# Weight gradients of a two-branch attention layer: transposes and gates at other places, two small gradients in one pass

## The chip, the cores and the metric

The kernel runs on one core of one Trainium2 chip. A core has a matrix engine (TensorE, PE in the profile, with its weight loads as PEld), a vector engine (VectorE, DVE), a scalar engine (ScalarE, ACT), a general engine (GpSimd, POOL) and a queue engine (SyncE, SP) that here only issues transfers. GpSimd issues transfers too. The transfers run on 16 DMA engines that all queues share. Each engine works through its own instructions in order; semaphores tie the engines together. The metric is the device time of one execution in microseconds (us).

## The reference

The reference computes a layer and all its gradients. For x (2048 tokens, 576 wide), the output is g * a + (1 - g) * b, where g is a sigmoid gate per token, a is attention with 32 query heads of 18 and one shared key and value head, and b is attention with 32 heads of 128 over 64 segments of 32 tokens, each with 8 memory rows that are handed on from segment to segment:

```
def _fwd_reference(A_x, A_wq, A_wk, A_wv, A_wo, B_x, B_mem0, B_Wq, B_Wk, B_Wv, B_Wo, B_seg_len, gate_w):
    ...
    g = _sigmoid((x * gate_w).sum(-1, keepdims=True))
    a = _A_ref(x, A_wq, A_wk, A_wv, A_wo)
    b = _B_ref(x, B_mem0, B_Wq, B_Wk, B_Wv, B_Wo, B_seg_len)
    return g * a + (1 - g) * b

def reference(A_x, ..., B_x, B_seg_len, grad_out):
    ...
    _out, _vjp = jax.vjp(_f, A_x, A_wq, A_wk, A_wv, A_wo, B_mem0, B_Wq, B_Wk, B_Wv, B_Wo, gate_w)
    return (out, *_vjp(grad_out))
```

The work around the change is the last of it: the gradients of the four large weights of branch b (each 576 x 4096), which are sums over 2048 tokens and 512 memory rows; the output itself with the gradient of the gate; and then the gradients of x and of the small weights of branch a (576 x 576 and 576 x 18).

## The kernel before, in words

The kernel runs in stages, one after the other: preparation, projections, the forward chain over segments woven with the first pass of branch a, the bulk of branch b, the backward chain woven with the second pass of branch a, a closing pass (`b_post`), the weight gradients (`b_dw`), and the final stage (`a_final`). The change lies in the last two. Their order of instructions is written out by hand (`manual_schedule`) in `b_dw`; in `a_final` a planner reorders what doesn't depend on each other.

`b_dw` has 16 sets, k = 0 to 15: four gradients (o, dq, dk, dv) times four pairs of 512 columns. A set's two tiles (w_d, for k = 0 w_a and w_b) have 20 blocks of 128 rows: 16 of tokens and 4 of memory rows. `load(k + 1)` is issued on SyncE at the head of set k; two tile pools alternate, so it waits until set k - 1 has released its tiles. For k < 4 the memory rows come by transposing transfers (`dma_start_transpose`). `groups` yields after every group: for k < 4 eight groups of 40 products of 288 columns, each in two accumulators, for k >= 4 eight groups of 20 products of 512 columns and a ninth in which the last 64 rows of both tiles run side by side (40 products, 64 columns of the array each). The accumulators (w_acc, six buffers) are evicted by VectorE and ScalarE in turn (`evac`), and the results leave by GpSimd's queue.

Between groups stands one step of a generator, `mem_tok`. It is made anew at k = 0, 4 and 8 and brings the memory rows' gradients (dq, dk, dv) into rows by token. Its start issues two loads (z_src, SyncE). Then for each of four blocks there is one step in which VectorE and GpSimd copy a half each (z_v, L612) and the next load but one is issued, and four steps of eight transposes on TensorE (z_pt), evicted to z_tk; the fourth writes the block to memory by GpSimd's queue (L623). So twenty steps, of which sixteen have work for TensorE. What is written for dq is read by `load(4)`.

At each set's end stands `gate(k)` for the token block k: ten products on TensorE (o_T by w_wo), then on VectorE the difference to branch b (o_diff), the output (o_out), the sum for the gate's gradient and its share of dz_all. Its inputs are fetched by `gate_load(k)` at the head of the set, behind `load(k + 1)`: o_b and o_go on GpSimd's queue, and o_T by a transposing transfer on SyncE's queue (L968). Each has one buffer, so the next set's fetch waits until this set's gate has read it. At k = 1 SyncE also fetches hx, the token and memory rows that serve from k = 4 on, ahead of o_T. After k = 15 dz_all is cast (w_dz) and 32 products give the gradient of gate_w (L1536 to L1545), and two large loads for the final stage (`ot`, `da`) are issued.

`a_final` first makes dx for each of 16 token blocks. Then, for each of five blocks of weight rows (four of 128, one of 64), it sums two gradients over 16 token blocks with `row_mm` (512 and 64 columns, accumulator f_big), evicts them and writes them by SyncE's queue (L2184), and a third, small one (f_pk), which the planner puts earlier.

Of the kernel before, what the change touches and what calls it, by code (L numbers as in the profile page):

```python
# [12 lines left out]
BF16 = mybir.dt.bfloat16  # L13
F32 = mybir.dt.float32
U16 = mybir.dt.uint16
U32 = mybir.dt.uint32
P = 128

D = 576
# [27 lines left out]
class Kern:  # L47
# [1381 lines left out]
    def b_dw(self, sp, A, wB, wH, ht, psum):  # L1429
        nc = self.nc  # L1430
        NTT = self.NTT
# [3 lines left out]
        def load(k):  # L1435
            which, jp = WS[k // 4], k % 4
            ts = []
            if k == 0:
                tiles = [[pA.tile([P, 4, 512], BF16, name=f"w_{w}{j}", bufs=1) for j in range(n // 4)] for w in "ba"][::-1]
            else:  # L1440
                tiles, full[k] = [], []
                for _ in range(2):
                    t = (wB if k % 2 else pA).tile([P, n, 512], BF16, name="w_d", bufs=2)
                    full[k].append(t)
                    tiles.append([t[:, j:j + 4, :] for j in range(0, n, 4)])
            for jc in (2 * jp, 2 * jp + 1):
                cs = slice(jc * 512, (jc + 1) * 512)
                t = tiles.pop(0)
                src = self.xtok[which][0:self.T, cs].rearrange("(n p) d -> p n d", p=P)
                if k == 0:  # L1450
                    for j in range(NTT // 4):
                        nc.sync.dma_start(t[j][:], src[:, 4 * j:4 * j + 4, :])
                else:
                    nc.sync.dma_start(full[k][jc % 2][:, 0:NTT, :], src)
                ts.append((t, cs))
                if k < 4:
                    for mt in range(self.NM // P):
                        nc.sync.dma_start_transpose(
                            t[NTT // 4][:, mt, :].rearrange("p (h e) -> p h e", e=E),
                            self.oh_dram[mt][:, 4 * jc:4 * jc + 4, :].rearrange("e h t -> e (h t)"))  # L1460
                else:
                    nc.sync.dma_start(t[NTT // 4][:, :, :], self.mtok[which][:, cs].rearrange("(n p) d -> p n d", p=P))
            return ts
# [40 lines left out]
        with self.tc.manual_schedule():  # L1504
            self.load_h(None, self.dm_dram, wH, ht)
            full = {}
            hold = ExitStack()
            pA = A("wA0", hold)
            nxt = load(0)
            wo = sp.tile([P, NKT, D], BF16, name="w_wo", bufs=1)  # L1510
            nc.vector.memset(wo[64:128, 4, :], 0.0)
            nc.gpsimd.dma_start(wo[:, 0:4, :], self.A_wo[0:512, :].rearrange("(k p) d -> p k d", p=P))
            nc.gpsimd.dma_start(wo[0:64, 4, :], self.A_wo[512:D, :])
            mem = None
            for k in range(16):
                ts = nxt
                if k % 4 == 0 and k < 12:
                    mem = self.mem_tok(k // 4, sp, psum, 2)
                    next(mem)
                if k == 1:  # L1520
                    hold.close()
                    pA = A("wA")
                if k < 15:
                    nxt = load(k + 1)
                if k == 1:
                    hx = self.load_h(self.A_x, self.mem_dram, sp)
                gl = self.gate_load(k, sp)
                if k == 15:
                    self.final_load(pA, wH)
                for _ in groups(k, ts, ht):  # L1530
                    next(mem, None)
                self.gate(k, gl, wo, sp, psum)
                if k == 3:
                    ht = hx
            dz16 = sp.tile([P, NTT], BF16, name="w_dz", bufs=1)
            nc.vector.tensor_copy(dz16[:], self.dz_all[:])  # L1536
            pg = [psum.tile([P, 512], F32, name="w_acc", bufs=6) for _ in range(2)]
            for tt in range(NTT):
                for hf in range(2):
                    self.mm(pg[hf][0:1, 0:288], lhsT=dz16[:, tt:tt + 1], rhs=ht[:, tt, 288 * hf:288 * hf + 288],  # L1540
                            start=(tt == 0), stop=(tt == NTT - 1))
            dg16 = sp.tile([P, 2, 288], BF16, name="w_dg", bufs=1)
            for hf in range(2):
                nc.vector.tensor_copy(dg16[0:1, hf, :], pg[hf][0:1, 0:288])
            nc.sync.dma_start(self.outs[11][None, :], dg16[0:1].rearrange("p a b -> p (a b)"))  # L1545
            self.ftok["x"] = ht
            self.final_tok(wB, ("ot", "da"))
# [590 lines left out]
    def a_final(self, sp, psum):  # L2138
        nc = self.nc
        T, NTT = self.T, self.NTT  # L2140
        gwb, wq, wkv, dkv = self.fin
        tok = self.ftok
        wqT = sp.tile([P, NKT, D], BF16, name="f_wqT", bufs=1)
        wkvT = sp.tile([P, D], BF16, name="f_wkvT", bufs=1)
        for kd in range(NKT):
            drows = KT_ROWS[kd]
            ptr = psum.tile([P, 640], BF16, name="f_wtr", bufs=1)
            for kt in range(NKT):
                rows = KT_ROWS[kt]
                self.tr(ptr[0:drows, kt * P:kt * P + rows], wq[0:rows, kt, kd * P:kd * P + drows], rows)  # L2150
            self.evac(wqT[0:drows, kd, :], ptr[0:drows, 0:D])
        ptr = psum.tile([P, 640], BF16, name="f_wtr", bufs=1)
        for kt in range(NKT):
            rows = KT_ROWS[kt]
            self.tr(ptr[:, kt * P:kt * P + rows], wkv[0:rows, kt, :], rows)
        self.evac(wkvT[:, :], ptr[:, 0:D])
        dkt = sp.tile([P, NTT, 36], BF16, name="f_dkt", bufs=1)
        for t4 in range(NTT // 4):
            pk = psum.tile([P, 4, 36], F32, name="f_pk", bufs=1)
            for j in range(4):  # L2160
                tt = t4 * 4 + j
                self.mm(pk[:, j, :], lhsT=dkv[:, tt * P:(tt + 1) * P], rhs=self.selkv[:, :])
            self.evac(dkt[:, t4 * 4:t4 * 4 + 4, :], pk[:])
        for tt in range(NTT):
            trows = slice(tt * P, (tt + 1) * P)
            dqT = self.tok_T(tok["dq"][:, tt, :], sp, psum, "f")
            pdx = psum.tile([P, 640], F32, name="f_big", bufs=2)
            self.row_mm(pdx, [(dqT[0:KT_ROWS[kt], kt, :], wqT[0:KT_ROWS[kt], kt, :]) for kt in range(NKT)]
                        + [(dkv[:, trows], wkvT[:, :])])
            dx32 = sp.tile([P, D], F32, name="f_dx32", bufs=2)  # L2170
            nc.vector.scalar_tensor_tensor(out=dx32[:, :], in0=gwb[:, :], scalar=self.dz_all[:, tt:tt + 1],
                                           in1=pdx[:, 0:D], op0=ALU.mult, op1=ALU.add)
            dx16 = sp.tile([P, D], BF16, name="f_dx16", bufs=2)
            nc.gpsimd.tensor_tensor(out=dx16[:, :], in0=dx32[:, :], in1=tok["dxb"][:, tt, :], op=ALU.add)
            (nc.sync if tt % 2 == 0 else nc.gpsimd).dma_start(self.outs[1][trows, :], dx16[:, :])
        for kt in range(NKT):
            drows = KT_ROWS[kt]
            cs = slice(kt * P, kt * P + drows)
            for (l, r, o) in (("x", "dq", 2), ("ot", "da", 5)):
                pw = psum.tile([P, 640], F32, name="f_big", bufs=2)  # L2180
                self.row_mm(pw[0:drows], [(tok[l][:, tt, cs], tok[r][:, tt, :]) for tt in range(NTT)])
                o16 = sp.tile([P, D], BF16, name="f_o16", bufs=2)
                self.evac(o16[0:drows, :], pw[0:drows, 0:D])
                nc.sync.dma_start(self.outs[o][cs, :], o16[0:drows, :])  # L2184
            pk = psum.tile([P, 4, 36], F32, name="f_pk", bufs=1)
            for tt in range(NTT):
                self.mm(pk[0:drows, 0, :], lhsT=tok["x"][:, tt, cs], rhs=dkt[:, tt, :], start=(tt == 0),
                        stop=(tt == NTT - 1))
            k16 = sp.tile([P, 36], BF16, name="f_k16", bufs=2)
            self.evac(k16[0:drows, :], pk[0:drows, 0, :])  # L2190
            nc.gpsimd.dma_start(self.outs[3][cs, :], k16[0:drows, 0:DA])
            nc.gpsimd.dma_start(self.outs[4][cs, :], k16[0:drows, DA:36])
# [159 lines left out]
```

## Time and profile before

| | us |
|---|---|
| median of three runs | 5294.08 |
| lowest and highest | 5291.89, 5295.3 |
| the profiled execution | 5284.42 |
| its span in the profile | 5282.7 |

| engine | busy us (share of the span) |
|---|---|
| PE | 4991.7 (94%) |
| DVE | 3589.8 (68%) |
| ACT | 3293.3 (62%) |
| POOL | 2553.9 (48%) |

The page shows one profiled execution. Times in its rows count from the start of the span. In a row of the timeline the first number is the start, the second the time until the last of the merged instructions ended, then follow engine, line, operation, the tile written and those read, sizes, count, and in brackets the engine's idle time before it with what ended it. Rows with SPq are SyncE issuing transfers; their time holds what the issue itself waited for, not the transfer. Matmuls overlap, so a group's time is best read from start to start. The stage `b_dw` begins at 4495.93 us in these rows, and `a_final` at 5187.23.

### The profile page before, as it was taken

The page shows a single profiled execution, that of the slowest core. Times are in us where ns is not written, and L with a number is a line of the kernel's source. Part 1 is how long each engine was busy: PE and PEld are TensorE (multiplying, and loading weights), DVE is VectorE, ACT ScalarE, POOL GpSimd, SP SyncE. Part 2 cuts the span into 40 slices and gives each one's busy share as a digit, 9 for nine tenths or more (in the row PEclk, how much of TensorE's full clock was granted, in tenths as well). Part 3 has the DMA queues.
Part 4 walks back from the last instruction along what each step waited for, and adds up shares of the span by engine and source line. Part 5 has one row for each costly group of instructions (what it writes and reads, how often), then busy time and mean ns, then how long its engine had stood idle before and what let it go on. Part 6 is the DMA issues. An engine that isn't in the chain of part 4 may idle for free.

```text
span 5282.7 us, 213348 instructions
## 1 busy us (share of the span) xinstructions
PE 4991.7 (94%) x90766; PEld 2902.2 (55%) x90945; DVE 3589.8 (68%) x7122; ACT 3293.3 (62%) x4757; POOL 2553.9 (48%) x4852
## 2 busy tenths in 40 slices
PE   7999999999999998999889999999999999999998
PEld 4335555555555555777645555555554467764444
DVE  5338888888888887777678888888888831111112
ACT  4228888888888885666668888888877732111100
POOL 3005555555555555767646666666654421222223
PEclk9999999999999999999999999999999999999999
DMA  7755666655665446888866989989877678966663
GB/s 227 241 193 134 145 143 140 146 139 139 146 141 128 121 105 193 254 245 250 264 171 179 201 195 198 198 202 198 201 163 148 139 178 221 275 221 213 195 184 102
DMA packets 1120042, 961.15 MB, mean 182 GB/s; under 512 B 689966, under 2 KB 948023, under 8 KB 1109486
## 3 DMA queue, kind: packets, MB, share of 16 engines
q1 hardware_dynamic: 1020398, 709.26, 54.6%
q0 software_dynamic: 98544, 238.08, 15.0%
q8 instruction: 712, 11.67, 1.0%
q14 instruction: 244, 2.00, 0.1%
q10 hardware_dynamic: 144, 0.15, 0.0%
HBM read 521.16 MB, written 357.96 MB: 166 GB/s over the span
## 4 chain that ended last, share of the span: by engine, by line
PE 69%; ACT 9%; issue 8%; DVE 5%; DMA 4%; POOL 4%; SPq 1%; POOLq 0%; ACTq 0%; DVEq 0%
PE w_acc L82 12%; PE r_pj L82 7%; PE b_S L82 6%; PE a_S L82 6%; PE a_acc L82 5%; ACT b_E L2052 5%; PE c_pj L82 5%; PE b_acc L82 5%; PE r_x L82 5%; PE p_pb L82 4%; PE c_x L82 4%; ACT a_E L1879 3%; PE x_tr L87 2%; PE f_big L82 1%; PE x_po L82 1%
## 5 line engine op out<-in xcount | busy, mean ns | idle before, releaser
L2075 DVE TENSOR_TENSOR b_dS<-b_dP,b_E 128x512 bf16<-128x512 f32 x2048 | 1315.1, 684 | 220.5 <-issue 88.9
L1912 DVE TENSOR_TENSOR a_W<-a_dP,a_E 128x512 bf16<-128x512 f32 x2048 | 1313.9, 684 | 204.6 <-issue 76.2
L2052 ACT ACTIVATE b_E<-b_S 128x1024 bf16<-128x1024 f32 x1024 | 1047.8, 1023 | 286.5 <-PE b_dP L82 200.4
L1879 ACT ACTIVATE a_E<-a_S 128x1024 bf16<-128x1024 f32 x1024 | 1049.0, 1024 | 237.2 <-PE a_dP L82 193.3
L82 PEld LDWEIGHTS <-b_QS 32*128 32x128 bf16 (+1 forms) x8192 | 271.4, 92 | 522.1 <-issue 466.3
L82 PE MATMUL r_pj<-WT,r_dT 128*32 128x288 bf16 x12288 | 495.6, 286 | 3.9 <-issue 3.9
L82 PE MATMUL b_S<-b_KV,b_QS 32*128 32x512 bf16 x2048 | 404.6, 382 | 94.3 <-ACT b_E L2052 60.9
L82 PE MATMUL w_acc<-w_d,w_h 128*128 128x512 bf16 (+1 forms) x2352 | 470.9, 379 | 2.5
L82 PE MATMUL a_S<-a_QD,l_KV 32*128 32x512 bf16 x2048 | 399.3, 381 | 41.6 <-ACT a_E L1879 19.8
L82 PE MATMUL b_acc<-b_dS,b_QS 128*32 128x512 bf16 x2048 | 423.5, 392 | 0.1
L82 PE MATMUL a_acc<-a_E,l_VK 128*32 128x256 bf16 x8192 | 412.3, 278 | 5.0
L82 PE MATMUL b_acc<-b_E,b_QS 128*32 128x512 bf16 x2048 | 405.9, 393 | 0.0
L82 PE MATMUL b_dP<-b_KV,b_QS 32*128 32x512 bf16 x2048 | 402.1, 387 | 0.0
L82 PE MATMUL a_dP<-a_QD,l_KV 32*128 32x512 bf16 x2048 | 398.4, 385 | 0.2 <-DVE a_W L1912 0.2
L82 PEld LDWEIGHTS <-r_dT 128*32 128x32 bf16 x12288 | 336.4, 97 | 93.3 <-issue 6.6
L82 PEld LDWEIGHTS <-w_h 128*128 128x128 bf16 (+1 forms) x2688 | 229.9, 100 | 258.5 <-issue 6.8
L82 PEld LDWEIGHTS <-l_KV 32*128 32x128 bf16 x4096 | 149.9, 91 | 287.0 <-issue 263.5
L82 PE MATMUL a_acc<-a_W,l_WK 128*32 128x256 bf16 x4096 | 291.5, 273 | 0.4 <-DVE a_W L1912 0.3
L79 ACT CAST w_o<-w_acc 128x512 bf16<-128x512 f32 x54 | 31.6, 585 | 384.7 <-PE w_acc L82 371.7
L82 PEld LDWEIGHTS <-l_VK 128*32 128x32 bf16 x8192 | 129.0, 94 | 237.1 <-issue 233.3
L77 DVE CAST w_o<-w_acc 128x512 bf16<-128x512 f32 x54 | 37.3, 692 | 325.2 <-PE w_acc L82 276.6
L1100 POOL TENSOR_TENSOR r_kb<-r_ks,bmask 128x512 bf16<-128x512 bf16 x176 | 188.7, 1072 | 103.7 <-DMA r_ks<-dsx_dram 39.2
(488 smaller groups left out, 10527.9 us busy)
## 6 DMA issues: line engine op xcount, KB each, us to landing
b_QS<-qs_dram SPq DMA_DIRECT2D x256, 256.0 KB
dOx_dram<-p_tok SPq DMA_DIRECT2D x16, 1024.0 KB
c_vx<-vx_dram SPq DMA_DIRECT2D x64, 256.0 KB
krow_dram<-c_k POOLq DMA_DIRECT2D x64, 256.0 KB
qrow_dram<-c_q POOLq DMA_DIRECT2D x64, 256.0 KB
vrow_dram<-c_v POOLq DMA_DIRECT2D x64, 256.0 KB
x_q<-qx_dram SPq DMA_DIRECT2D x32, 512.0 KB
x_k<-kx_dram SPq DMA_DIRECT2D x32, 512.0 KB
```

The source lines that it names most:

```text
L77: nc.vector.tensor_copy(out, in_)
L79: nc.scalar.copy(out, in_)
L82: return self.nc.tensor.matmul(out, lhsT, rhs, start=start, stop=stop, tile_position=tp, skip_group_check=True)
L87: return self.nc.tensor.transpose(out, in_, self.identB[b:b + nrows, b:b + nrows], tile_position=tp)
L1100: nc.gpsimd.tensor_tensor(out=B[:], in0=a[:].unsqueeze(2).to_broadcast([P, 4, 4, SEG]), in1=self.bmask[:, :, 0].unsqueeze(1).unsqueeze(3). ...
L1879: nc.scalar.activation(E_[n][:], S.pop(n)[:], ACT.Exp, scale=SCALEA)
L1912: nc.vector.tensor_tensor(out=W_[n][:, i, :], in0=dP[i][:], in1=E_[n][:, i, :], op=ALU.mult)
L2052: nc.scalar.activation(E_[n][:], S.pop(n)[:], ACT.Exp, scale=SCALEA)
L2075: nc.vector.tensor_tensor(out=D_[n][:, i, :], in0=dP[i][:], in1=E_[n][:, i, :], op=ALU.mult)
```

## The change

Three edits. In set 0 the first three groups are no longer followed by a step of `mem_tok`, so all its twenty steps for dq come three groups later (five in set 0, eight in set 1, seven in set 2, where there were eight, eight and four). For k = 1 to 15 `gate(k)` stands behind the seventh group's step instead of at the end: one group earlier for k < 4, two groups earlier for k >= 4; for k = 0 it stays behind the eighth. In the final stage the 64-row block's two gradients are computed into the two halves of one accumulator, by products that alternate between the two column halves of the array, with one eviction and one output each on SyncE's and on GpSimd's queue.

```
-                for _ in groups(k, ts, ht):
-                    next(mem, None)
-                self.gate(k, gl, wo, sp, psum)
+                for i, _ in enumerate(groups(k, ts, ht)):
+                    if k or i > 2:
+                        next(mem, None)
+                    if i == 7 - (k > 0):
+                        self.gate(k, gl, wo, sp, psum)
                 if k == 3:
                     ht = hx
...
+        pairs = (("x", "dq", 2), ("ot", "da", 5))
         for kt in range(NKT):
             drows = KT_ROWS[kt]
             cs = slice(kt * P, kt * P + drows)
-            for (l, r, o) in (("x", "dq", 2), ("ot", "da", 5)):
+            if drows == 64:
+                pw = psum.tile([P, 640], F32, name="f_big", bufs=2)
+                for c in (slice(0, 512), slice(512, D)):
+                    for tt in range(NTT):
+                        for i, (l, r, o) in enumerate(pairs):
+                            self.mm(pw[64 * i:64 * i + 64, c], lhsT=tok[l][:, tt, cs], rhs=tok[r][:, tt, c],
+                                    start=(tt == 0), stop=(tt == NTT - 1), tp=(0, 64 * i))
+                o16 = sp.tile([P, D], BF16, name="f_o16", bufs=2)
+                self.evac(o16[:], pw[:, 0:D])
+                for i, (l, r, o) in enumerate(pairs):
+                    (nc.sync, nc.gpsimd)[i].dma_start(self.outs[o][cs, :], o16[64 * i:64 * i + 64, :])
+            for (l, r, o) in pairs if drows == P else ():
                 pw = psum.tile([P, 640], F32, name="f_big", bufs=2)
```

With the change, SyncE's queue differs in one place: the load of the dq generator's fourth block stands behind k = 1's o_T instead of behind k = 0's.

## Prediction

> **What bounds the kernel now.** I read the page first, then the chain that ended last, then, stage by stage, TensorE's and SyncE's rows in order of time in the last 800 us, where all edits lie.
>
> ```profile
> PE 4991.7 (94%) x90766; PEld 2902.2 (55%) x90945; DVE 3589.8 (68%) x7122; ACT 3293.3 (62%) x4757; POOL 2553.9 (48%) x4852
> PE w_acc L82 12%; PE r_pj L82 7%; PE b_S L82 6%; PE a_S L82 6%; PE a_acc L82 5%; ACT b_E L2052 5%; PE c_pj L82 5%; PE b_acc L82 5%; PE r_x L82 5%; PE p_pb L82 4%; PE c_x L82 4%; ACT a_E L1879 3%; PE x_tr L87 2%; PE f_big L82 1%; PE x_po L82 1%
> ```
>
> TensorE is busy 94% of the span, and the weight gradients' products (w_acc) are the largest part of the chain. So an edit in that stage is worth what it takes from or adds to TensorE's idle time, its clock, or its number of passes. Its rows at the start of the stage:
>
> ```profile
> 4495.93 9.96 PE L82 MATMUL w_acc<-w_h,w_a 128*128 128x288 bf16 x80
> 4514.80 0.61 PE L87 MATMUL z_pt<-identB,z_v 128*128 128x128 bf16 x4 [8.91 <-DVE z_v L612]
> 4516.55 0.61 PE L87 MATMUL z_pt<-identB,z_v 128*128 128x128 bf16 x4 [1.14 <-POOL z_v L612]
> 4516.95 6.67 PE L82 MATMUL w_acc<-w_h,w_a 128*128 128x288 bf16 x40
> 4523.45 0.61 PE L87 MATMUL z_pt<-identB,z_v 128*128 128x128 bf16 x8
> 4523.90 5.06 PE L82 MATMUL w_acc<-w_h,w_a 128*128 128x288 bf16 x40
> 4528.80 0.61 PE L87 MATMUL z_pt<-identB,z_v 128*128 128x128 bf16 x8
> 4529.24 5.06 PE L82 MATMUL w_acc<-w_h,w_b 128*128 128x288 bf16 x40
> ...
> 4550.18 1.39 PE L82 MATMUL w_acc<-w_wo,o_T 128*128 128x288 bf16 x10
> ...
> 4593.29 1.39 PE L82 MATMUL w_acc<-w_wo,o_T 128*128 128x288 bf16 x10
> 4594.51 5.06 PE L82 MATMUL w_acc<-w_h,w_d 128*128 128x288 bf16 x40
> ```
>
> In full flow a group of 40 products takes 4.90 us (4523.90 to 4528.80) and a step of eight transposes 0.44. Two groups run, then TensorE waits 8.91 and 1.14 us for the first copy of memory gradients, and the next group is slow. SyncE's queue, one row of GpSimd's, and the DMA load in the same stretch (columns after the stretch: its length, busy us of PE, PEld, DVE, ACT, POOL, then clock, DMA share, GB/s):
>
> ```profile
> 4532.87 1.28 SPq L968 DMA_TRANSPOSE o_T<-otok_dram  x1
> ...
> 4549.93 0.37 SPq L1454 DMA_DIRECT2D w_d<-ox_dram  x1
> ...
> 4577.87 0.58 SPq L1424 DMA_DIRECT2D w_h<-in_A_x_dram  x1
> ...
> 4581.95 4.32 SPq L968 DMA_TRANSPOSE o_T<-otok_dram  x1
> ```
> ```profile
> 4536.10 0.54 POOL L623 DMA_DIRECT2D dqm_dram<-z_tk  x1
> ```
> ```profile
> 4505.90:4516.90 11.00, 0.96 (x8) 0.70 (x9) 1.06 (x2) 0.40 (x1) 2.82 (x2) 0.69 1.08 323
> 4516.90:4537.00 20.10, 20.10 (x167) 15.83 (x165) 2.75 (x5) 3.22 (x5) 2.25 (x5) 0.92 1.20 286
> 4537.00:4540.00 3.00, 3.00 (x27) 2.38 (x26) 0.38 (x2) 0.27 (x1) 0.00 (x0) 1.00 0.98 393
> 4540.00:4549.90 9.90, 9.90 (x89) 8.03 (x87) 1.83 (x4) 0.57 (x3) 2.98 (x3) 1.00 0.59 220
> 4549.90:4560.00 10.10, 10.10 (x93) 8.23 (x91) 4.16 (x10) 1.77 (x3) 2.69 (x5) 1.00 1.04 265
> 4580.00:4592.00 12.00, 12.00 (x109) 9.76 (x107) 1.61 (x3) 1.81 (x3) 1.62 (x3) 1.00 1.04 312
> ```
>
> The DMA engines are full (share about 1) except from 4540 to 4550, where SyncE waits for a z_src buffer and then for the first set's tiles. So the first sets stand close to a second bound, the loads.
>
> **Part 1, the transposes three groups later (k = 0).** Nothing is removed. TensorE runs groups 0 to 4 from 4495.93 and comes to the transposes at 4495.93 + 5 x 4.90 = 4520.4. In the rows above, VectorE's copy was done by 4514.80 and GpSimd's by 4516.55. In the new order both stand behind the eviction and output of group 3 (products done 4515.5), so VectorE's is ready by about 4517 and GpSimd's, 1.75 later above, by 4519. No wait is left. Group 4 needs the second tile set (w_b), whose loads stand ahead of z_src in SyncE's queue; z_src had been read by 4514.8, so w_b should be there at 4515.5. The worth: from 4495.93 to 4523.45 three groups and one step took 27.52 us, in flow 3 x 4.90 + 0.44 = 15.14: **-12.4 us**. It holds the idle 10.05, the slow group (6.67 for 5.06: the clock column shows 0.69) and slow transposes.
>
> What the earlier TensorE then meets: the gate of k = 0. With four steps instead of six in this set it comes at 4495.93 + 8 x 4.90 + 4 x 0.44 = 4536.9 instead of 4550.18. Its input o_T was issued by SyncE until 4534.15, and outputs now leave earlier and share the DMA engines. Between no wait and 2 us, I take **+1** (nearest row: the DMA share is 1.20 just there).
>
> The steps moved out of this set go through the next two; the last write of dq's memory rows comes three groups later, some 16 us, and SyncE's read of it (k = 4's load, then that set's o_T and two z_src) queues behind. TensorE needs them from 4677.15:
>
> ```profile
> 4627.80 0.36 SPq L1462 DMA_DIRECT2D w_d<-dqm_dram  x1
> 4638.32 4.33 SPq L968 DMA_TRANSPOSE o_T<-otok_dram  x1
> 4677.15 8.80 PE L82 MATMUL w_acc<-w_d,w_h 128*128 128x512 bf16 x39
> ```
>
> 4627.8 + 16 leaves 30 us: nothing. z_src for the fourth block now queues behind k = 1's o_T, and is needed only three groups into k = 2: nothing.
>
> **Part 2, the gates ahead.** For k = 1 to 15 the ten products (1.24 us) only change place. VectorE's six operations fit between evictions. But the inputs are needed one group earlier for k < 4 (4.90 + 0.44 us) and two groups for k >= 4 (8.8 to 9.7 us). GpSimd's queue has the gate's output ahead of the last groups' outputs, which wait for nothing it delays.
>
> k = 1 is the tight one. o_T was issued until 4581.95 + 4.32 = 4586.27 and used without a wait at 4593.29. So from SyncE's start of the third load (4549.93) to its landing passed 36.3 to 43.3 us, with DMA full. That load starts when k = 0's last group releases its tiles, now at 4536.5. The same time gives 4572.8 to 4579.8. Two transfers are in the way that were done before: z_src until about 4540 (+3.5, the row of 4537 to 4540 at 393 GB/s) and the first block of memory rows (128 x 4096 bf16, 1 MB), whose write was issued at 4536.10 and now near 4538 (+4.0 at the 265 GB/s of 4549.9 to 4560). So 4580 to 4587, or, with the two absorbed by the idle rate (220 against up to 393 GB/s), 4573. TensorE arrives at about 4537.9 + 1.2 + 7 x 4.90 + 5 x 0.44 = 4575.6. The wait lies between 0 and 11; I take **+6**, the middle, since the full DMA rows are the nearest.
>
> Everything behind it on TensorE waits too, and the clock follows. What an idle time costs in clock the end of the stage shows:
>
> ```profile
> 5175.62 1.40 PE L82 MATMUL w_acc<-w_wo,o_T 128*128 128x288 bf16 x10
> 5179.82 7.00 PE L82 MATMUL w_acc<-w_h,w_dz 128*1 128x288 bf16 x32 [2.80 <-DVE w_dz L1536]
> ...
> 5187.23 0.52 PE L87 MATMUL f_wtr<-identB,w_h 128*128 128x128 bf16 x5 [0.41 <-DVE w_dg L1544]
> 4856.14 0.40 PE L87 MATMUL z_pt<-identB,z_v 128*128 128x128 bf16 x4 [1.61 <-POOL z_v L612]
> ```
> ```profile
> 5179.80:5186.80 7.00, 6.98 (x32) 3.69 (x33) 0.07 (x1) 0.00 (x0) 0.00 (x0) 0.57 0.05 21
> ```
>
> After 2.80 us of idle time the clock was 0.57 over the next 7 us, and 32 products took 6.9 us that at the gate's pace (1.24 for ten) take 4.0. So a wait of 2.8 us or more costs about 2.5 more: **+2.5** (0 if the wait is short, 3 at most). The Trainium skill, "TensorE: Matmul & The Clock Gate", section "What's actually happening", says that the clock halves after an idle window of about 3.4 us and returns after about as much busy time. By that page this 2.80 us gap need not have halved the clock, and a return after 3.4 us would cost 1.7; the sum would be 0.8 lower at k = 1. Here the shorter gap did it, and I go by the row.
>
> For k = 15 the edit removes that stall: dz is ready two groups early, so the 2.80 go, and the 32 products run in 4.0 instead of 6.9: **-5.7**. Late next is the copy of the two results before f_wtr (0.41), as before.
>
> For k = 2 to 14 the slack is larger. The worst of the later sets is k = 6:
>
> ```profile
> 4775.39 6.04 SPq L968 DMA_TRANSPOSE o_T<-otok_dram  x1
> 4803.97 1.40 PE L82 MATMUL w_acc<-w_wo,o_T 128*128 128x288 bf16 x10
> ```
>
> The issue ends at 4781.43 and the gate moves to about 4795.2: 13.7 us, where k = 1 shows that 7.0 suffice. Nothing. At k = 8 GpSimd's copy kept TensorE 1.61 us; its queue is ordered anew there, so between 0 and -1.6, I take **-0.8**.
>
> **Part 3, the last 64 rows side by side.**
>
> ```profile
> 4714.46 4.51 PE L82 MATMUL w_acc<-w_d,w_h 128*64 128x512 bf16 x40
> 4734.42 4.48 PE L82 MATMUL w_acc<-w_d,w_h 128*128 128x512 bf16 x20
> 5270.55 4.14 PE L82 MATMUL f_big<-w_d,w_h 128*64 128x512 bf16 x32
> 5274.53 4.12 PE L82 MATMUL f_big<-w_d 128*64 128x512 bf16 x32
> 5274.79 0.75 DVE L77 CAST f_o<-f_big 64x576 bf16<-64x576 f32 x1 [3.32 <-PE f_big L82]
> 5278.70 0.63 ACT L79 CAST f_o<-f_big 64x576 bf16<-64x576 f32 x1 [11.32 <-PE f_big L82]
> ```
>
> The 40 half-width products of the weight stage take the time of 20 full ones, so neighbours run together. The same pairing holds here: 64 products, 8.1 us. The 32 wide ones become 16 pairs of 0.22, 3.6; the 32 of 64 columns take 0.5 in pairs (3.98 per gradient less 16 x 0.216 for the wide ones) or 1.0 one by one. So 4.1 to 4.6: -3.5 to -4.0. One eviction, on VectorE now, 0.75 for 0.63: +0.1. Its two outputs go by SyncE and GpSimd; the second path's tail I bound at 0 to +0.5, from the 0.54 us of GpSimd's issue above. All this is the path to the end: **-3.4**.
>
> **Sum** against the profiled execution (5284.42 us, span 5282.7): -12.4 + 1 + 6 + 2.5 - 5.7 - 0.8 - 3.4 = -12.8, so 5271.6. The runs' median is 5294.08, 9.7 above that execution; the same difference gives **5281 us**.
>
> **The rivals.**
> - *Inputs in time.* o_T of k = 1 lands before 4575.6, no wait and no half clock: -12.4 + 1 - 5.7 - 0.8 - 3.4 = -21.3, 5273. For it: the idle DMA share of 0.59 from 4540 to 4550 can be used now. Against: full shares on both sides of it.
> - *The wait moves to the gate.* The half clock comes and the wait is 11 or, with the slow transposing loads near 4560 to 4570 repeated, a little more: what the first part gains is spent and the ends remain: -7.8 at a wait of 11, 5286, and 5287 or more with those; no measurable change. For it: k = 1's 7 us between issue and use.
> - *The later gates come too early*, the one on the other side. From k = 5 to 14 the gate needs o_T 9 us sooner; if it lands so late that each waits, the ten sets pay each time. It decides from landings 13 us after the end of the issue. At 2 us each, +20 - 12.8 = +7, 5301; from 2.8 us with the clock, over +40. Against: the 7.0 us of k = 1.
> - *The pairs don't overlap*, or GpSimd's output ends late: 3.4 us less gain, 5285; within the range.
>
> **How the numbers follow.** Forecast 0.50 (own range 5276 to 5286), inputs in time 0.20, wait moved 0.17, late gates 0.08, pairs 0.05. The point is the forecast's; the range 5270 to 5290 takes in the second and third and leaves out the fourth and a spread of runs. The bound of 0.2% is 10.6 us, about what a measurement of this kernel can tell, at 5283.5: the forecast lies beyond it in some seven of ten, inputs in time always: 0.35 + 0.20 = 0.55, and a little of the last. Same: the rest of the forecast, the moved wait and the pairs. Slower: late gates and a small part for what no row shows.
>
> **What would show it.** In the new profile: no idle time ahead of z_pt at the start and full clock there; a wait ahead of the second gate's products (w_wo, o_T), with half clock behind it; none ahead of gates 2 to 14; w_dz straight after the last group in 4 us; one pair block of 4.1 to 4.6 us at the end. The prediction is wrong if the second gate doesn't wait, if a later one does, or if group 4 waits for w_b.

## The result and the profile after

The changed kernel takes 5287.05 us (median of 20 runs) against 5297.66 for the kernel before (20 runs). The ratio of their times is 0.9981, with a 95% interval of 0.9973 to 0.9988: 0.12 to 0.27% faster, some 10 us. The forecast was 12.8 us (0.24%) faster, and the range held the time. Its point, 5281 us, was counted from a median of three runs that is 3.6 us below the one of twenty. By the bound of 0.2% that the prediction named, the result lies just inside "same", for which it had given less than for "faster".

The profiled execution of the changed kernel has a span of 5274.6 us (before: 5282.7). A span alone says little here: the weight gradients' first product starts at 4502.84 us, where it started at 4495.93 before, in code that the change doesn't touch. In the ten profiles of this case that start lies between 4495.9 and 4514.4. So all that follows is counted from that first product to the end of the span: **786.8 us before, 771.8 after, -15.0**.

TensorE's timeline of the changed kernel, at the start of the stage and at the second gate (start, time, engine, line, operation, tiles, sizes, count, idle time before and what ended it):

```profile
4502.84 19.76 PE L82 MATMUL w_acc<-w_h,w_a 128*128 128x288 bf16 x160
4522.44 5.06 PE L82 MATMUL w_acc<-w_h,w_b 128*128 128x288 bf16 x40
4527.34 0.61 PE L87 MATMUL z_pt<-identB,z_v 128*128 128x128 bf16 x8
...
4544.57 1.40 PE L82 MATMUL w_acc<-w_wo,o_T 128*128 128x288 bf16 x10 [0.58 <-DMA o_T<-otok_dram]
...
4581.89 0.61 PE L87 MATMUL z_pt<-identB,z_v 128*128 128x128 bf16 x8
4586.35 2.58 PE L82 MATMUL w_acc<-w_wo,o_T 128*128 128x288 bf16 x10 [3.84 <-DMA o_T<-otok_dram]
4588.72 5.37 PE L82 MATMUL w_acc<-w_h,w_d 128*128 128x288 bf16 x40
4593.93 0.61 PE L87 MATMUL z_pt<-identB,z_v 128*128 128x128 bf16 x8
...
4677.90 8.80 PE L82 MATMUL w_acc<-w_d,w_h 128*128 128x512 bf16 x40
...
4856.89 0.40 PE L87 MATMUL z_pt<-identB,z_v 128*128 128x128 bf16 x4 [1.61 <-POOL z_v L612]
```

Five groups run without a gap, and the wait of 8.91 and 1.14 us ahead of the first transposes is gone. A new one stands ahead of the second gate: 3.84 us, ended by o_T's transfer. Behind it the gate's ten products take 2.37 us from start to start instead of 1.23. The changed kernel's stretches over that place (length, busy us of PE, PEld, DVE, ACT and POOL, then granted clock, DMA share and GB/s):

```profile
4582.50:4585.90 3.40, 0.00 (x1) 0.00 (x0) 0.69 (x1) 0.04 (x1) 0.54 (x1) 1.00 1.21 243
4585.93:4589.34 3.41, 3.00 (x13) 1.93 (x14) 0.62 (x2) 0.00 (x0) 0.00 (x0) 0.50 0.98 382
4589.35:4592.70 3.35, 3.35 (x29) 2.64 (x28) 1.92 (x6) 0.00 (x0) 0.54 (x1) 1.00 1.10 351
```

While TensorE is idle the clock is still 1.00; then it is 0.50 for 3.41 us. The end of the stage and the last block:

```profile
5177.60 4.08 PE L82 MATMUL w_acc<-w_h,w_dz 128*1 128x288 bf16 x32
5182.45 0.52 PE L87 MATMUL f_wtr<-identB,w_h 128*128 128x128 bf16 x5 [0.78 <-DVE w_dg L1546]
...
5203.28 2.01 PE L82 MATMUL f_big<-f_wqT,f_T 128*128 128x512 bf16 x5 [3.06 <-DVE f_T L77]
...
5264.91 0.40 PE L82 MATMUL f_big<-w_d,w_h 128*64 128x512 bf16 x1
5264.91 0.40 PE L82 MATMUL f_big<-w_d 128*64 128x512 bf16 x1
...
5268.86 0.20 PE L82 MATMUL f_big<-w_d,w_h 128*64 128x64 bf16 x1
5268.86 0.20 PE L82 MATMUL f_big<-w_d 128*64 128x64 bf16 x1
```

The gate weight's products (w_dz) have no idle time before them and take 4.1 us; f_wtr, behind them, are the final stage's first transposes. The two small gradients' products start at the same time in pairs, and all 64 are done in 4.15 us.

| step, from start to start in the rows | forecast | measured |
|---|---|---|
| to the first gate's products, incl. its wait (54.25 before, 41.73 after; 0.9 of transposes only moved on) | -11.4 | -11.6 |
| wait ahead of the second gate | +6 | +3.84 |
| half clock behind it (1.14 at the gate, 0.31 in the next group) | +2.5 | +1.45 |
| sum up to the fifth set (181.22 before, 175.06 after) | -2.9 | -6.2 |
| wait of 1.61 at k = 8 | -0.8 | 0 |
| k = 15: idle time, and products to f_wtr (7.41 before, 4.85 after) | -5.7 | -5.5 |
| dx in the final stage (83.3 before, 82.5 after) | 0 | -0.9 |
| last block to the end (12.15 before, 9.7 after) | -3.4 | -2.4 |
| sum | -12.8 | -15.0 |

### The profile page after: what moved, and what is told of

The parts are those of the page before. It is cut to its first block, busy times and chain, and to the rows that moved or that the text cites. A ratio compares the mean times of both kernels' runs of the same rounds, so it can differ in the third digit from the quotient of the medians.

```text
span 5274.6 us, 213519 instructions
## 1 busy us (share of the span) xinstructions
PE 4994.6 (95%) x90945; PEld 2898.4 (55%) x90945; DVE 3589.9 (68%) x7121; ACT 3295.0 (62%) x4757; POOL 2553.8 (48%) x4853
## 4 chain that ended last, share of the span: by engine, by line
PE 71%; ACT 9%; issue 5%; DVE 4%; DMA 4%; POOL 3%; SPq 1%; POOLq 0%; ACTq 0%; DVEq 0%
PE w_acc L82 11%; PE r_pj L82 7%; PE b_S L82 6%; PE a_S L82 6%; ACT b_E L2054 5%; PE a_acc L82 5%; PE c_pj L82 5%; PE b_acc L82 5%; PE r_x L82 5%; PE p_pb L82 4%; PE c_x L82 4%; ACT a_E L1881 3%; PE y_pdx L82 2%; PE x_tr L87 2%; PE x_po L82 1%
```

## The experiments

**The first part alone.** The question was whether the new wait comes from the loads as such or from the gate's place.

```
-                for _ in groups(k, ts, ht):
-                    next(mem, None)
+                for i, _ in enumerate(groups(k, ts, ht)):
+                    if k or i > 2:
+                        next(mem, None)
                 self.gate(k, gl, wo, sp, psum)
```

> The first part alone: transposes three groups later, every gate at its set's end, the final stage as before. Counted from the stage's first product to the end of the span, before took 786.8 us and the changed kernel 771.8. Theory (the wait ahead of the second gate comes from moving that gate one group forward): TensorE comes to the second gate 5.3 us later than in the changed kernel, o_T has landed, no wait; 786.8 - 12.4 + 0.6 for the first gate = 775.0. Rival (the loads bound the first two sets wherever the gate stands): 2 us or more of wait at the second gate or in the third set, 778 to 782.

Measured: 771.1 us from the first product (4503.37) to the end (5274.5); ratio 0.9973 (0.9961 to 0.9984). No wait above 0.2 us at either of the first two gates. TensorE's timeline of this run, at the second gate and at the end of the stage:

```profile
4587.20 0.61 PE L87 MATMUL z_pt<-identB,z_v 128*128 128x128 bf16 x8
4587.65 1.39 PE L82 MATMUL w_acc<-w_wo,o_T 128*128 128x288 bf16 x10
...
5175.06 4.08 PE L82 MATMUL w_acc<-w_h,w_dz 128*1 128x288 bf16 x32 [2.79 <-DVE w_dz L1537]
5179.92 0.52 PE L87 MATMUL f_wtr<-identB,w_h 128*128 128x128 bf16 x5 [0.78 <-DVE w_dg L1545]
```

At its set's end the gate finds o_T landed: the theory holds and the loads are not a bound by themselves. The stretch is 3.9 us shorter than expected. The end shows most of it, 2.6 us, and dx in the final stage another 1.1: the idle time ahead of the gate weight's products is there (2.79 us), but they run at full speed, 4.86 us to f_wtr where before took 7.41. So the prediction's "idle time of 2.8 us costs 2.5 more" isn't a constant.

**The second part alone.**

```
-                for _ in groups(k, ts, ht):
+                for i, _ in enumerate(groups(k, ts, ht)):
                     next(mem, None)
-                self.gate(k, gl, wo, sp, psum)
+                    if i == 7 - (k > 0):
+                        self.gate(k, gl, wo, sp, psum)
```

> The second part alone: gates one or two groups ahead for k = 1 to 15, transposes and final stage as before. Theory (the wait is the gate's own place): o_T of k = 1 is used 5.3 us sooner than before, so TensorE waits 2 to 5 us there although the first stall of 8.9 and 1.1 us is still present, and loses about 1.4 to the half clock; at k = 15 the 2.8 us and the slow products go, -5.5. Together 786.8 + 5 - 5.5 = 786 from the stage's first product to the end. Rival (the wait comes from the first part, TensorE arriving 12 us sooner): no wait at the second gate, 781.

Measured: 786.3 us (4497.56 to 5283.8). The first stall is there as before, and yet:

```profile
4589.64 0.61 PE L87 MATMUL z_pt<-identB,z_v 128*128 128x128 bf16 x8
4594.20 2.58 PE L82 MATMUL w_acc<-w_wo,o_T 128*128 128x288 bf16 x10 [3.95 <-DMA o_T<-otok_dram]
```

The wait at the second gate is 3.95 us without the first part, 3.84 with it. It belongs to the gate's place and not to the first part: TensorE's earlier arrival brings the loads forward by as much, since they start when TensorE releases tiles (the third load starts 40.7 us behind the first product with the first part and 54.1 without, and the gate's wait ends at 83.5 and 96.6). The runs give a ratio of 0.9987 (0.9976 to 0.9998), a few us faster, where this stretch shows no gain; that difference is not explained by the profiles, and the spread of the stages before is larger.

**The queue's order.** In the changed kernel, at k = 1:

```
-                if k == 1:
-                    hx = self.load_h(self.A_x, self.mem_dram, sp)
                 gl = self.gate_load(k, sp)
+                if k == 1:
+                    hx = self.load_h(self.A_x, self.mem_dram, sp)
```

> The changed kernel with one exchange at k = 1: the gate's inputs are fetched ahead of the two loads into hx (2.3 and 0.6 MB) instead of behind them. Theory (o_T is late because it stands behind hx in SyncE's queue): it lands some 9 us sooner, the wait of 3.84 us and the 1.4 us of half clock at the second gate go, 771.8 - 5.2 = 766.6 from the stage's first product to the end. Rival (the DMA engines as a whole are the bound, so the wait only moves to tiles or to the next gate): 770 to 772.

Measured: 766.6 us (4508.28 to 5274.8), and no wait above 0.3 us at any gate. SyncE's rows, first of the changed kernel, then of this run:

```profile
4570.26 0.58 SPq L1424 DMA_DIRECT2D w_h<-in_A_x_dram  x1
4570.87 1.96 SPq L1426 DMA_DIRECT2D w_h<-mem_dram  x1
4572.93 6.72 SPq L968 DMA_TRANSPOSE o_T<-otok_dram  x1
```
```profile
4575.70 1.21 SPq L968 DMA_TRANSPOSE o_T<-otok_dram  x1
4576.96 0.58 SPq L1424 DMA_DIRECT2D w_h<-in_A_x_dram  x1
4577.58 5.87 SPq L1426 DMA_DIRECT2D w_h<-mem_dram  x1
```

Counted from each run's first product, o_T's issue ends at 76.8 us in the changed kernel and at 68.6 here. The wait doesn't move anywhere else. Up to the fifth set the stretch is 5.9 us shorter than the changed kernel's; dx gives 0.65 back, with half clock for 6.8 us where the changed kernel had 3.4, so the exact hit of 766.6 is in part luck. The cause is the place behind hx in one queue, and the rival of an overall DMA bound falls. The ratio to before is 0.9956 (0.9944 to 0.9968).

**Both outputs by SyncE's queue.** The run above, and in the final stage:

```
-                    (nc.sync, nc.gpsimd)[i].dma_start(self.outs[o][cs, :], o16[64 * i:64 * i + 64, :])
+                    nc.sync.dma_start(self.outs[o][cs, :], o16[64 * i:64 * i + 64, :])
```

> As the run with the gate's inputs ahead of hx, and the two outputs of the last 64 rows both go by SyncE's queue. Theory (GpSimd's late transfer keeps that engine's closing drain 1.4 us longer than SyncE's landing): another -1.2 us, 765.4 from the stage's first product to the end. Rival (the last landing alone sets the end): 766.6 or slightly more, since the second issue stands behind the first.

Measured: 766.3 us (4505.12 to 5271.4). The end alone fits the theory: 8.7 us from the last block's first product, 9.7 with GpSimd's queue. But the first gate waited 1.04 us in this execution (0.58 in the changed kernel, 0.3 in the run above), which takes the gain back in this profile. The ratio is 0.9949 (0.9932 to 0.9967), 5271.15 against 5297.79: this version beats the kernel before and, as the intervals lie apart (0.9973 to 0.9988 there), the changed kernel. Against the run above the intervals overlap.

**The third part alone, in three forms.** First as in the change:

> The third part alone. Read from the first product of the 64-row block to the end of the span: before 12.15 us, changed kernel 9.73. Theory (the block's time is independent of the rest): 9.7. It also has the stall of 2.8 us ahead of the gate weight's products. Theory of fixed cost (2.8 us idle halves the clock for some 7 us): 7.4 us from those products' start to the final stage's first transpose, as before. Theory of free windows (the clock is judged in windows of about 3.4 us whose phase differs between executions, so the gap counts only where it fills most of one): 7.4 in some executions, 4.9 in others, as the first run showed 4.9 after 2.79 us idle.

Then with both outputs by SyncE's queue (the edit of the run above):

> The third part alone, both outputs by SyncE's queue. Theory (GpSimd's closing drain behind its late transfer costs the end about 1 us): 8.7 us from the first product of the 64-row block to the end, 1.0 less than with one output on GpSimd's queue. Rival (the end follows the last landing): 9.7. For the 2.8 us stall as in the run of the third part alone: 7.4 us by the fixed cost, 7.4 or 4.9 by free windows.

And with the order of the products changed:

```
-                for c in (slice(0, 512), slice(512, D)):
-                    for tt in range(NTT):
-                        for i, (l, r, o) in enumerate(pairs):
+                for i, (l, r, o) in enumerate(pairs):
+                    for c in (slice(0, 512), slice(512, D)):
+                        for tt in range(NTT):
```

> The third part alone, but the products of the first gradient all ahead of those of the second, still in the two column halves of one accumulator with one eviction. Theory (only neighbours in the instruction order run together): the 64 products take 8.0 us instead of 4.2, so 13.5 us from the block's first product to the end, worse than before's 12.15. Rival (the halves overlap whatever the order): 9.7. For the 2.8 us stall as in the run of the third part alone.

These three were run once each, so only the stretches are read and not the whole times. Measured from the block's first product to the end: 10.1, 9.0 and 13.9 us, each 0.3 to 0.4 more than expected. In the last run the products stand one behind the other:

```profile
5285.36 4.05 PE L82 MATMUL f_big<-w_d,w_h 128*64 128x512 bf16 x29
5289.22 0.40 PE L82 MATMUL f_big<-w_d 128*64 128x512 bf16 x1
5289.24 0.26 PE L82 MATMUL f_big<-w_d,w_h 128*64 128x64 bf16 x3
5289.46 3.91 PE L82 MATMUL f_big<-w_d 128*64 128x512 bf16 x31
```

So 8.0 us for the 64 products instead of 4.15: here the halves of the array share time only where neighbours in the order use different halves, and with that order the edit costs 1.8 us instead of saving 2. For the end, SyncE's issue rows of the first and the second form:

```profile
5290.71 0.52 SPq L2190 DMA_DIRECT2D out_dram<-f_o  x1
```
```profile
5276.45 1.16 SPq L2190 DMA_DIRECT2D out_dram<-f_o  x2
```

From the issue to the end of the span (5295.8 and 5280.5) it is 5.1 us with one output on GpSimd's queue and 4.1 with both on SyncE's. Together with the pair above (9.7 and 8.7) the 1.0 us is seen twice; one form differs by up to 0.4 between executions. GpSimd's closing drain is what ends late: it takes 3.60 to 3.66 us in all ten traces, and it starts with GpSimd's last issue. In the changed kernel that is at 5270.18, so it ends at 5273.84, while SyncE's closing waits are over at 5272.5; without an output on its queue GpSimd starts it some 30 to 40 us ahead of the end. What the drain itself waits for, no trace shows.

All three have the 2.8 us stall ahead of the gate weight's products, with nothing different ahead of it. TensorE's timeline of the first form and of the second:

```profile
5198.30 4.08 PE L82 MATMUL w_acc<-w_h,w_dz 128*1 128x288 bf16 x32 [2.80 <-DVE w_dz L1536]
```
```profile
5182.72 5.75 PE L82 MATMUL w_acc<-w_h,w_dz 128*1 128x288 bf16 x32 [2.79 <-DVE w_dz L1536]
```

And a stretch of each behind that gap (columns as in the stretches further up), of the first form, the second and, last, the kernel before:

```profile
5198.30:5202.80 4.50, 4.09 (x33) 2.70 (x34) 0.51 (x2) 0.00 (x0) 0.00 (x0) 1.00 0.08 33
```
```profile
5182.82:5186.19 3.37, 3.37 (x15) 1.77 (x14) 0.00 (x0) 0.00 (x0) 0.00 (x0) 0.50 0.11 44
```
```profile
5178.99:5185.80 6.81, 5.98 (x26) 3.13 (x27) 0.70 (x5) 0.00 (x0) 0.48 (x1) 0.50 0.06 22
```

The same gap is followed by no half clock, by 3.4 us of it, and by 6.8 us of it. In the five executions that have it the products take, up to f_wtr, 7.4 (before), 4.9 (the first part alone), 4.5, 6.2 and 6.0 us. The fixed cost falls.

The free windows can be looked at directly. But for the last one, which the end cuts off, every stretch of half clock in the ten traces is a whole multiple of 3.41 us long. So each trace can be cut into stretches of that length, counted from an edge of its own half clock. The stretch that ends within or behind the gap, of the second form, the last form, the kernel before, the first part alone and the first form:

```profile
5179.34:5182.75 3.41, 0.61 (x6) 0.26 (x5) 2.72 (x8) 0.00 (x0) 1.65 (x3) 1.00 0.18 41
5193.09:5196.51 3.42, 1.02 (x9) 0.59 (x6) 2.41 (x7) 0.39 (x1) 1.60 (x3) 1.00 0.18 41
5175.57:5178.98 3.41, 1.45 (x12) 0.90 (x10) 2.01 (x4) 0.59 (x1) 1.15 (x3) 1.00 0.17 41
5173.07:5176.48 3.41, 1.42 (x12) 1.00 (x13) 1.87 (x6) 0.00 (x0) 0.56 (x1) 1.00 0.26 77
5193.76:5197.18 3.42, 1.74 (x14) 0.90 (x10) 1.73 (x4) 0.59 (x1) 1.08 (x2) 1.00 0.18 41
```

Behind the first three, in which TensorE was busy for 0.61, 1.02 and 1.45 us, the clock was halved; behind the last two, with 1.42 and 1.74, it was not. So what counts is how much of the gap falls into one stretch, and that differs between executions. The bound lies near 1.4 us of work; these five don't give it more exactly.

**The second gate one more group forward.** The suspected wait enlarged:

```
-                    if i == 7 - (k > 0):
+                    if i == 7 - (k > 0) - (k == 1):
```

> The changed kernel with the gate of k = 1 one more group forward (behind the sixth group's step instead of the seventh's). Theory (o_T's landing is set by the loads, not by TensorE): the wait grows by the group and its step, 3.84 + 4.90 + 0.44 = 9.2 us, and the stage is 5.3 us longer (771.8 to 777.1 from its first product to the end), up to 3.4 more if the half clock lasts two windows more. Rival (the loads wait on TensorE's progress too, so o_T comes sooner or later with it): a wait under 7 or over 11 us.

TensorE's timeline at the second gate, and the stretch at half clock:

```profile
4589.65 2.58 PE L82 MATMUL w_acc<-w_wo,o_T 128*128 128x288 bf16 x10 [9.10 <-DMA o_T<-otok_dram]
4592.03 6.42 PE L82 MATMUL w_acc<-w_h,w_d 128*128 128x288 bf16 x40
```
```profile
4584.56:4594.80 10.24, 5.15 (x22) 3.30 (x23) 2.54 (x7) 0.00 (x0) 0.54 (x1) 0.50 1.09 339
```

In this one execution the wait is 9.10 us, and the stretch 778.3 (4505.58 to 5283.9), 6.5 longer than the changed kernel's. The wait ends 84.1 us behind the first product, in the changed kernel 83.5: o_T lands when the queue brings it, wherever TensorE stands. The next group is slower too (6.26 from start to start for 4.90), since the half clock lasted 10.24 us.

## Why the prediction was right, and where it was not

*The first part* came as worked out: the stall is gone, group 4 didn't wait for w_b, and the first gate waits 0.58 us (forecast 1, in other runs 0.2 to 1.2).

*The new wait at the second gate* was named with its place, its cause and its sign. Its size, "I take +6, the middle", was 3.84. The step that failed is the two transfers "in the way that were done before": the second part alone has neither, and waits 3.95. SyncE starts the third load at k = 1 in these rows, first of the changed kernel, then of the second part alone:

```profile
4543.57 0.36 SPq L1454 DMA_DIRECT2D w_d<-ox_dram  x1
```
```profile
4551.62 0.37 SPq L1454 DMA_DIRECT2D w_d<-ox_dram  x1
```

From there to the end of the wait passed 42.8 and 42.6 us: the two transfers cost nothing that can be seen, and both times lie at the upper end of the 36.3 to 43.3 that the prediction read from before. That range by itself puts o_T between 4572.8 and 4579.8 and the wait, for a gate at 4575.6, between 0 and 4.2 us. o_T's lateness is that of the queue before the change; in it the gate, by these times, had 0.6 to 0.8 us to spare, and the move took a whole group of 4.90.

*The clock's cost* was mis-sized in one term and by its kind in another. The Trainium skill, "TensorE: Matmul & The Clock Gate", section "What's actually happening", has the clock judged in free-running windows of 3413 ns. The traces agree on the windows: half clock in the rows above lasts 3.41, 6.81 or 10.24 us, and it begins at different places of the same gap. A whole idle window, which the prediction quotes from the Trainium skill, wasn't needed to halve it: 1.45 us of work in a window of 3.41 didn't prevent it.

The prediction went by the row of one execution and made it a fixed 2.5. By the traces a wait costs half of the time at half clock in which TensorE works. At the second gate that is one window less the 0.42 us of it that were still idle, 1.5 by this and 1.45 measured. A gap of 2.80 us costs nothing or up to 2.9, by the execution. Of the -5.5 at k = 15 only the 2.80 is sure; that the rest came as forecast is luck of the two executions compared. The -0.9 in dx is of this sort too: its wait (3.06 for 3.19) stayed, the half clock behind it shortened (3.4 us for 6.8).

*The last block* paired as forecast (4.15 for 4.1 to 4.6). The forecast's 0 to 0.5 for GpSimd's path was too low: 1.0, and -2.4 for -3.4 in all.

*At k = 8* the middle of 0 and -1.6 was taken; it is 0. GpSimd's queue order there wasn't what held the copy.

*The sum* was -12.8, the stretch gave -15.0, the runs some -10. That it came so near is in part luck: single terms missed by up to 2.2 us, some one way and some the other. With the clock's share of chance (up to 2.6 at k = 15 and 0.9 in dx) the stretch alone gives -11.5 to -15, within the runs' interval of -6.4 to -14.3 or just beyond it.

What the change's parts are worth by themselves: the first -12.2 up to the fifth set (its ratio alone, 0.9973, is no worse than the 0.9981 of the whole change, with intervals that overlap), the third about 2, and the second is spent: 2.8 and a chance of clock gained at the end, 3.9 and the clock behind it lost at the second gate. One exchange in a queue makes it pay.

## What to carry to other kernels

When work is moved ahead, look up when its inputs land, not only whether it waited before: no idle time ahead of it can mean one microsecond of slack, and a load that nobody waits for (here 2.9 MB that serve three sets later) may stand ahead of it in the queue. Count from a fixed event near the change to the end, since the stages before differ between executions by more than the effect. Don't take the clock's cost of a short gap from one execution.

## What the runs showed of the hardware that was not expected

The clock was at half for 3.41 or 6.81 us behind an idle time of 2.80 us, and not at all behind the same 2.80 us in two of five executions; behind 3.84 us it was at half for 3.41 us, and behind 9.10 us for 10.24. Products in the two halves of the array overlapped only as neighbours in the order (4.15 against 8.0 us for 64). A last output on GpSimd's queue instead of SyncE's ended the execution 1.0 us later, in two pairs of runs, with GpSimd's closing drain of 3.6 us behind it.
